# Layer A scores: one 80-column product, or three of 32, 32 and 16 columns

## The chip, the cores and the metric

The kernel runs on one core of one Trainium2 chip. Its time is in device microseconds (us); the figure for a kernel is the median of its runs. One execution is also taken by the hardware profiler, and everything said below of single instructions comes from that one. Engines: PE is TensorE's matmul, PEld its weight load, DVE VectorE, ACT ScalarE, POOL GpSimd, SP SyncE, which issues most of the DMAs. In this kernel a product on PE is always a pair of instructions: LDWEIGHTS brings the stationary operand (rows x columns, as in `128*32`), MATMUL streams the moving operand through it (`128x384`: 384 columns).

## The reference

Four layers, A, B, A, B, each added to its input after a layer norm. Layer A is attention with a memory: the 2048 tokens go in 64 segments of 32, one behind the other, and each segment carries 8 memory rows that are the first 8 output rows of the segment before. So a segment can't be finished before the one ahead of it. Layer B is a linear attention over all tokens. The change is in layer A alone, which is (shortened):

```python
for s in range(n_seg):                               # 64 segments of 32 tokens
    h = jnp.concatenate([mem, xs], axis=1)           # 8 + 32 rows, 640 wide
    q = jnp.einsum('btd,dhe->bhte', h, Wq)           # 32 heads of 192
    k = jnp.einsum('btd,dhe->bhte', h, Wk)
    v = jnp.einsum('btd,dhe->bhte', h, Wv)
    scores = jnp.einsum('bhqe,bhke->bhqk', q, k) * scale
    scores = jnp.where(mask[None, None], scores, -1000000000.0)
    p = _softmax(scores, axis=-1)
    o = jnp.einsum('bhqk,bhke->bhqe', p, v)
    o = jnp.einsum('bhte,hed->btd', o, Wo)
    mem = o[:, :M, :].copy()                         # 8 rows for the next segment
    outs.append(o[:, M:, :])
```

The mask lets everyone see the 8 memory rows, and lets a query see a key that does not come after it.

## The kernel before

Before a chain of segments starts, everything that does not depend on the memory rows is computed for all segments at once and kept in DRAM: the queries and keys of the last 8 tokens of each segment (`kqb`) and their values (`vb`). What is left is `A_chain`, the serial part: 64 segments per layer, each of 4 rounds of 8 heads. Even segments take the rounds as 0, 1, 2, 3, odd ones backwards, so that the weights of the turning round can stay. "Round 0" below is the first in time.

**The work of a round on PE**, in the order in which it is written in the segment loop (the loop over `n` at L1302):

- `project` (L1075, its matmul L1092): q, k or v of 32 rows (8 memory rows and 24 tokens). 5 pieces of the contraction, 640 = 5 x 128, times 4 column groups of 32 columns (`tile_position=(0, 32*g)`), each streaming 384 columns: 20 products, in quads.
- `scores` (L1123, matmul L1129): keys of a chunk, all 128 rows and 80 columns wide, are stationary, and the queries of that chunk, 80 columns, stream. 8 products per round, two accumulated for each of four results. The 80 columns are 64 of two heads' own keys (32 rows each) and 16 of the last tokens of both. This matmul names no column group.
- `attend` (L1135, matmul L1142, result `ps_o`) multiplies the weights E with the values, 8 products of 193 columns on four column groups, and `attend_tails` (L1149, L1155, `ps_t`) does it for the last tokens' queries, 4 products.
- `wo_round` (L1193, L1198, `ps_w`) multiplies the outputs of earlier rounds with Wo, in column groups as well; some of it stands between scores and projections as filling.

The order on PE in a segment is: Q, K, V of round 0; then for rounds 0, 1, 2: Q of the next round, scores of this round, (in round 1, 16 products of L1198), K of the next round, `ps_o`, `ps_t` (rounds 0 and 1) or 8 products of L1198 (round 2), V of the next round; then scores of round 3, the tails of round 2, 20 products of L1198, `ps_o` and `ps_t` of round 3, and the last 52 products of L1198. The result `ps_w` is turned by DVE (L1371), added into the next segment's `hT` (L1373), and the next segment's Q starts.

**Beside PE.** ACT copies a projected q or k from PSUM to `raws` (`to_rows`, L1107), DVE turns it into `QK` (`turn_rows`, L1112): `KT` and `QT` are the two halves of that tile. POOL copies the last tokens' queries and keys into the same tile (`extra_kq`, L1069). So scores read columns 0 to 63 from DVE's turn and 64 to 79 from POOL's copy. ACT's exponential (`weigh`, L1218) reads all of the scores' PSUM tile `ps_s` and writes E, which `attend` loads as stationary. DVE takes the reciprocals (L1162, L1166), ACT scales (L1172), DVE turns the result for `wo_round`.

**What sets the order around the change.** The order of instructions is written out by hand (a manual schedule), engine by engine; waits are added from what each tile's writers and readers are. An instruction that needs more than one wait gets a standalone wait instruction ahead of it on its engine.

**Weights.** Not all of layer A's weights stay on the chip. In each segment SP brings seven pieces of 384 KB into `slot` tiles (three of Wq, two of Wk, two of Wv, for the last round) and four of 320 KB of Wo. `PACE` says after which step of a projection each of the eleven may be issued; the last Wv piece is tied to the Q projection of round 2, the last Wo piece to the K projection of round 3. All go through one queue of SP.

Of the kernel before, what the change touches and what calls it, by code (L numbers as in the profile page):

```python
# [125 lines left out]
class Kernel:  # L126
# [876 lines left out]
    def A_chain(self, xn_dram, at_dram, li, load_slot, piece, late_wo, load_both, wo, low):  # L1003
        nc, tc, KC, NSEG = self.nc, self.tc, self.KC, self.NSEG
        scale = float(self.Dh) ** -0.5
        NR = 4
        with tc.tile_pool(name=f"A{li}_ch", reuse_waits="tile", bufs=1) as sp, \
# [4 lines left out]
            KT, QT = QK[:, 0], QK[:, 1]  # L1012
# [110 lines left out]
            def scores():  # L1123

                S = pop.tile([P, 512], F32, name="ps_s", tag="s")
                for x in range(2):
                    for c in range(4):
                        c0 = 160 * x + 80 * (c // 2)
                        nc.tensor.matmul(S[0:80, c0:c0 + 80], lhsT=KT[:, 4 * x + c, :], rhs=QT[:, 4 * x + c, :],  # L1129
                                         start=(c % 2 == 0), stop=(c % 2 == 1), skip_group_check=True)  # L1130
                return S

            pair = [None]
# [79 lines left out]
            def weigh(E_before=None):  # L1213
                S = scores()
                if E_before is not None:
                    attend_tails(E_before, 2)
                E = sp.tile([P, 320], BF16, name="E", tag="E")
                nc.scalar.activation(out=E[0:80, 0:320], in_=S[0:80, 0:320], func=ACT.Exp, scale=scale)  # L1218
                return E
# [249 lines left out]
```

## Time and profile before

| what | value |
|---|---|
| median of 3 runs | 3266.28 us (3250.03 to 3268.61) |
| the profiled execution: span from its first to its last instruction | 3253.7 us |
| mean granted TensorE clock | 0.994 |
| layer A's two chains in the span, about | 178 to 1380 and 1760 to 2997 us |
| L1129: weight loads and products | 4096 and 4096 |
| duration of one L1129 load and product, median | 123 and 207 ns |
| DMA packets, bytes | 325018, 747.58 MB |

How to read the lines that follow: a group line has the source line, the engine, the operation, what it writes and reads by the program's names, the shape (stationary rows*columns, then the moving operand), the count, the busy time, the mean of one, and the idle time of the engine just before with what ended most of it. A line of the order of time has a start, a length, the engine and the group, and in brackets an idle time before it and who ended it. The end of a matmul is modelled and its pipelined tail overlaps the next one, so the pace of products is read from starts. The page holds the span alone, no time around it.

### The profile page before, as it was taken

The page shows a single profiled execution, that of the slowest core. Times are in us where ns is not written, and L with a number is a line of the kernel's source. Part 1 is how long each engine was busy: PE and PEld are TensorE (multiplying, and loading weights), DVE is VectorE, ACT ScalarE, POOL GpSimd, SP SyncE. Part 2 cuts the span into 40 slices and gives each one's busy share as a digit, 9 for nine tenths or more (in the row PEclk, how much of TensorE's full clock was granted, in tenths as well). Part 3 has the DMA queues.
Part 4 walks back from the last instruction along what each step waited for, and adds up shares of the span by engine and source line. Part 5 has one row for each costly group of instructions (what it writes and reads, how often), then busy time and mean ns, then how long its engine had stood idle before and what let it go on. Part 6 is the DMA issues. An engine that isn't in the chain of part 4 may idle for free.

```text
span 3253.7 us, 140890 instructions
## 1 busy us (share of the span) xinstructions
PE 3095.3 (95%) x59424; PEld 1980.2 (61%) x59730; DVE 2208.8 (68%) x5457; ACT 1883.0 (58%) x4481; POOL 1410.7 (43%) x2920
## 2 busy tenths in 40 slices
PE   9989999999999999999999899999999999999999
PEld 7756666666666666555367566666666666665553
DVE  5557777777777777666643577777777777776465
ACT  3346666666666666646433466666666666666453
POOL 3345555555455455430122355555555554554300
PEclk9999999999999999999999999999999999999999
DMA  8977777777777777840385677777777777778400
GB/s 306 372 271 253 256 248 257 232 255 253 236 256 245 244 257 238 285 166 1 113 319 193 240 233 257 248 252 256 242 264 240 259 244 245 255 236 282 149 1 33
DMA packets 325018, 747.58 MB, mean 230 GB/s; under 512 B 65818, under 2 KB 100274, under 8 KB 321314
## 3 DMA queue, kind: packets, MB, share of 16 engines
q1 hardware_dynamic: 254850, 638.55, 56.1%
q0 software_dynamic: 67616, 86.77, 9.7%
q10 hardware_dynamic: 1920, 13.24, 1.0%
q8 instruction: 469, 7.68, 1.0%
q14 instruction: 163, 1.34, 0.1%
HBM read 668.80 MB, written 77.03 MB: 229 GB/s over the span
## 4 chain that ended last, share of the span: by engine, by line
PE 75%; DMA 11%; DVE 8%; issue 3%; ACT 3%; POOL 0%; SPq 0%; PEld 0%; DVEq 0%; POOLq 0%; ACTq 0%
PE ps_qk_q L1092 12%; PE ps_qk_k L1092 12%; PE ps_v L1092 11%; PE ps_w L1198 10%; DMA arena<-in_A_Wv_dram 6%; PE ps_pre L960 6%; PE ps_s L1129 5%; PE ps_o L1142 3%; PE ps_pre L989 3%; PE kv L1424 2%; DVE raws L1371 2%; PE ps_wo L444 2%; DMA Vp<-vb 2%; DMA arena<-wo_rows 2%; DVE hT L1373 2%
## 5 line engine op out<-in xcount | busy, mean ns | idle before, releaser
L1092 PEld LDWEIGHTS <-hT 128*32 128x32 bf16 x30720 | 792.6, 97 | 422.7 <-issue 43.0
L1112 DVE STREAM_TRANSPOSE QK<-raws 128x512 bf16<-128x512 bf16 (+1 forms) x1152 | 730.7, 643 | 207.3 <-ACT raws L1107 166.7
L1092 PE MATMUL ps_qk_q<-arena,hT 128*32 128x384 bf16 x10240 | 510.4, 327 | 38.2 <-DVE hT L1373 31.1
L1069 POOL COPY QK<-kqb 64x192 bf16<-64x192 bf16 x1024 | 350.4, 342 | 380.9 <-PE ps_s L1129 344.3
L1092 PE MATMUL ps_qk_k<-arena,hT 128*32 128x384 bf16 x10240 | 511.7, 328 | 3.1 <-issue 1.2
L1107 ACT ACTIVATE raws<-ps_qk_k 128x512 bf16<-128x512 f32 (+1 forms) x640 | 313.5, 510 | 253.1 <-PE ps_qk_k L1092 253.1
L1092 PE MATMUL ps_v<-arena,hT 128*32 128x384 bf16 x8192 | 435.2, 326 | 15.2 <-DMA arena<-in_A_Wv_dram 7.2
L1073 POOL DMA_DIRECT2D Vp<-vb x512 | 257.6, 503 | 416.3 <-PE ps_t L1155 252.0
L1172 ACT ACTIVATE raws<-ps_o,rc 128x192 bf16<-128x192 f32 x1024 | 373.4, 420 | 109.3 <-DVE rc L1166 104.8
L1107 ACT ACTIVATE raws<-ps_qk_q 128x512 bf16<-128x512 f32 x512 | 305.7, 597 | 164.5 <-PE ps_qk_q L1092 153.4
L1198 PE MATMUL ps_w<-arena,under 128*32 128x320 bf16 x6144 | 307.4, 300 | 16.7 <-issue 13.1
L1062 POOL DMA_DIRECT2D kqb<-kqb x512 | 290.6, 568 | 70.2 <-POOL QK L1069 50.2
L1121 DVE CAST Vp<-ps_v 64x384 bf16<-64x384 f32 x512 | 286.4, 559 | 37.9 <-ACT Vp L1119 22.8
L1129 PEld LDWEIGHTS <-QK 128*80 128x80 bf16 x4096 | 195.8, 121 | 161.4 <-issue 157.3
L1119 ACT ACTIVATE Vp<-ps_v 64x384 bf16<-64x384 f32 x512 | 246.4, 481 | 55.5 <-PE ps_v L1092 54.2
L1129 PE MATMUL ps_s<-QK 128*80 128x80 bf16 x4096 | 256.8, 210 | 5.4 <-POOL QK L1069 2.8
L1218 ACT ACTIVATE E<-ps_s 80x320 bf16<-80x320 f32 x512 | 217.6, 425 | 32.3 <-PE ps_t L1155 28.9
L1051 ACT ACTIVATE wh<-ps_w 64x160 f32<-64x160 f32 x256 | 76.6, 299 | 264.8 <-DVE raws L1371 254.9
L1058 POOL DMA_DIRECT2D attn<-under x128 | 91.6, 716 | 292.8 <-DVE under L1054 289.7
L960 PEld LDWEIGHTS <-arena 128*128 128x128 bf16 x1920 | 188.4, 98 | 32.4 <-DVE next_xT L97 4.6
L97 DVE CAST arena<-ps_pre 128x512 bf16<-128x512 f32 (+1 forms) x160 | 102.2, 646 | 143.5 <-PE ps_pre L960 96.4
L1142 PE MATMUL ps_o<-Vp,E 80*32 80x193 bf16 x4096 | 180.3, 248 | 13.2 <-DMA Vp<-vb 3.7
(159 smaller groups left out, 4586.2 us busy)
## 6 DMA issues: line engine op xcount, KB each, us to landing
arena<-wo_rows SPq DMA_DIRECT2D x560, 320.0 KB, 5.6
arena<-in_A_Wq_dram SPq DMA_DIRECT2D x427, 384.0 KB, 4.3
arena<-in_A_Wk_dram SPq DMA_DIRECT2D x298, 384.0 KB, 4.8
arena<-in_A_Wv_dram SPq DMA_DIRECT2D x290, 384.0 KB, 6.0
kqb<-kqb POOLq DMA_DIRECT2D x512, 48.0 KB, 4.9
vb<-arena POOLq DMA_DIRECT2D x128, 97.0 KB, 6.1
Vp<-vb POOLq DMA_DIRECT2D x512, 24.2 KB, 4.0
kqb<-arena SPq DMA_DIRECT2D x8, 1536.0 KB, 10.0
```

Source lines behind the costliest of these rows:

```text
L960: nc.tensor.matmul(ps[:, T * i:T * i + T], lhsT=w[b][:, P * c:P * c + P], rhs=xBT[:, b, :], start=(b == 0), stop=(b == KC - 1))
L1062: nc.gpsimd.dma_start(out=kqb[:], in_=self.kqb_d[r, :, s, :])
L1069: nc.gpsimd.tensor_copy(out=o, in_=kqb[h, :].rearrange("p (x c q) -> p x c q", c=3, q=16))
L1073: nc.gpsimd.dma_start(out=Vs[n % 2][64:80, :], in_=self.vb_d[s, r].rearrange("g t f -> (g t) f"))
L1092: last = nc.tensor.matmul(o, lhsT=hT[:, b, :], rhs=rhs, start=(i == 0), stop=(i == KC - 1), tile_position=(0, 32 * g), skip_group_check=True)
L1107: nc.scalar.activation(out=raw[:, c], in_=ps[:, c], func=ACT.Copy)
L1112: nc.vector.transpose(out=o, in_=i)
L1121: nc.vector.tensor_copy(out=o, in_=i)
L1129: nc.tensor.matmul(S[0:80, c0:c0 + 80], lhsT=KT[:, 4 * x + c, :], rhs=QT[:, 4 * x + c, :], start=(c % 2 == 0), stop=(c % 2 == 1), skip_gro ...
L1142: nc.tensor.matmul(O[G][32 * h:32 * h + 32, VH * G:VH * G + 193], lhsT=E[0:80, 80 * h + 32 * G:80 * h + 32 * G + 32], rhs=V[0:80, VH * h:V ...
L1172: nc.scalar.activation(out=out, in_=i, func=ACT.Copy, scale=rc[G])
L1198: step = nc.tensor.matmul(W[q:q + 32, 0:320], lhsT=OT[i // 6][:, i % 6 // 2, 32 * (i % 2):32 * (i % 2) + 32], rhs=rhs, start=(first and i ...
```

## The change

Each 80-column product of `scores` is split into three: stationary columns 0 to 31, 32 to 63 and 64 to 79, each on its own column group and each writing its own rows of the same PSUM tile. All three stream the same 80 query columns. The first two hold the two heads' own keys, the third the last tokens' keys. Result, PSUM tile, accumulation over the two chunks and readers stay.

```diff
                 for x in range(2):
                     for c in range(4):
                         c0 = 160 * x + 80 * (c // 2)
-                        nc.tensor.matmul(S[0:80, c0:c0 + 80], lhsT=KT[:, 4 * x + c, :], rhs=QT[:, 4 * x + c, :],
-                                         start=(c % 2 == 0), stop=(c % 2 == 1), skip_group_check=True)
+                        for g, m in enumerate((32, 32, 16)):
+                            nc.tensor.matmul(S[32 * g:32 * g + m, c0:c0 + 80], lhsT=KT[:, 4 * x + c, 32 * g:32 * g + m],
+                                             rhs=QT[:, 4 * x + c, :], start=(c % 2 == 0), stop=(c % 2 == 1),
+                                             tile_position=(0, 32 * g), skip_group_check=True)
                 return S
```

No other line of the kernel differs.

## The prediction

> **What bounds the kernel now.** I read the page's busy shares, then its chain, then PE's order of time around one block of scores, then ACT's, then the waits of the products behind the scores, then DMA shares over one segment.
>
> ```profile
> PE 3095.3 (95%) x59424; PEld 1980.2 (61%) x59730; DVE 2208.8 (68%) x5457; ACT 1883.0 (58%) x4481; POOL 1410.7 (43%) x2920
> ...
> PE 75%; DMA 11%; DVE 8%; issue 3%; ACT 3%; POOL 0%; SPq 0%; PEld 0%; DVEq 0%; POOLq 0%; ACTq 0%
> PE ps_qk_q L1092 12%; PE ps_qk_k L1092 12%; PE ps_v L1092 11%; PE ps_w L1198 10%; DMA arena<-in_A_Wv_dram 6%; PE ps_pre L960 6%; PE ps_s L1129 5%; PE ps_o L1142 3%; PE ps_pre L989 3%; PE kv L1424 2%; DVE raws L1371 2%; PE ps_wo L444 2%; DMA Vp<-vb 2%; DMA arena<-wo_rows 2%; DVE hT L1373 2%
> ...
> L1129 PE MATMUL ps_s<-QK 128*80 128x80 bf16 x4096 | 256.8, 210 | 5.4 <-POOL QK L1069 2.8
> ```
>
> PE bounds it, but 6% of the chain is the streamed Wv: a second bound lies close. Scores are 5%. What a block costs is read from starts, since busy time counts pipelined tails:
>
> ```profile
> 1003.58 0.99 PE L1092 MATMUL ps_v<-arena,hT 128*32 128x384 bf16 x20
> 1004.39 0.99 PE L1092 MATMUL ps_qk_q<-arena,hT 128*32 128x384 bf16 x20
> 1005.31 0.50 PE L1129 MATMUL ps_s<-QK 128*80 128x80 bf16 x8
> 1005.73 1.00 PE L1092 MATMUL ps_qk_k<-arena,hT 128*32 128x384 bf16 x20
> 1006.56 0.34 PE L1142 MATMUL ps_o<-Vp,E 80*32 80x193 bf16 x8
> 1006.73 0.26 PE L1155 MATMUL ps_t<-Vp,E 80*32 80x193 bf16 x4
> 1006.81 0.34 PE L1092 MATMUL ps_v<-arena,hT 128*32 128x384 bf16 x4
> ```
>
> A projection of 20 takes 0.81 us to the next start when another projection or a 193-wide product follows, 0.92 when scores follow; the scores take 0.42. In single records (medians over 118 inner segments): entry gap 0.104 us (0.916 against 0.812); eight score starts about 0.038 apart, the second 0.059 after the first; then 0.135 from the last score start to the next product, of which 0.038 is its own, so an exit gap of 0.098. Both gaps stand in all four rounds, and the exit is the same before projections, output products and tails. The entry gap can't be the DVE wait there: in rounds 1 and 2 the keys are ready 0.417 us before the first score. So I read both as the array running empty between full-width (80 columns) and 32-column work; 32-column work of other widths follows other 32-column work with no gap.
>
> **The change, part by part.** *Products.* 512 blocks (4 rounds x 64 segments x 2 layers) of 8 loads and 8 products become 24 and 24. No row shows 80-wide products on three column groups, so bounds: four groups run at once on the other rows (384 wide: a quad each 0.1625 us; 193 wide: 0.0825; thus 2.4 columns per ns plus 2 ns), which gives 80/2.4 + 2 = 36 ns per triple; from above, the present 80-column pair's 38 ns (its load is more than twice as wide) is near, and three 21 ns shares of a ps_o quad (63 ns) far. I take 36: it scales the same form of work. A block is then 8 x 0.036 = 0.288 instead of 0.428, and both gaps go (the exit is inside the 0.428): 0.104 + 0.140 = 0.244 us. Projections straight behind scores, 0.823 now, become 0.812 (rounds 0 and 2).
>
> *Waits.* In the built programs, PE's standalone wait ahead of a block (x512 on L1129) is now for DVE's turned keys; after the change it is for the scores before last written, over 110 instructions earlier, and the DVE wait sits on the first weight load. In round 0 the standalone wait ended 0.122 us before the first score, so it would have held the start; a wait carried by a load (E's, at L1142) releases it 0.05 us after its releaser. DVE ends 0.162 (round 0) and 0.147 to 0.274 (round 3) before the present first score, so a start 0.104 earlier still fits. Only PE's own order stands behind that wait.
>
> *What is late next: E.* ACT's order of time around the same block, and last the wait of the ps_o loads (us, times):
>
> ```profile
> 1005.43 0.60 ACT L1107 ACTIVATE raws<-ps_qk_q 128x512 bf16<-128x512 f32 x1 [0.33 <-PE ps_qk_q L1092]
> 1005.92 0.42 ACT L1218 ACTIVATE E<-ps_s 80x320 bf16<-80x320 f32 x1
> ...
>   ACT E L1218: 35.1, 112
> ```
>
> ACT evicts Q first, so in rounds 0 to 2 the exponential starts behind that, not behind the scores: faster scores do not bring E. The first ps_o product starts 0.214 (round 0), 0.71 (1), 0.139 (2) after E's end, and could start 0.054 after it. So round 0 keeps 0.16 of its 0.255, round 1 all 0.244, round 2 0.085. In round 3 E waits for the tails' products (L1155), which move with PE, so all 0.244. Sum 0.733 us per segment, 128 segments: 94 us, if weights were there.
>
> *Weights.* They are not: stretches of one segment, which starts at 1001.94, and last PE's wait in it:
>
> ```profile
> 1003.44:1006.44 3.00, 3.00 (x76) 1.91 (x72) 2.37 (x4) 2.21 (x5) 1.50 (x4) 1.00 0.88 276
> 1006.44:1009.44 3.00, 3.00 (x84) 2.04 (x80) 2.37 (x6) 2.31 (x6) 1.55 (x4) 1.00 0.96 343
> 1009.44:1012.44 3.00, 3.00 (x83) 1.92 (x76) 2.09 (x6) 2.06 (x6) 1.41 (x3) 1.00 0.97 300
> 1012.44:1015.94 3.50, 2.91 (x60) 1.58 (x60) 2.96 (x7) 2.19 (x7) 1.76 (x4) 1.00 1.00 371
> 1015.94:1020.30 4.36, 3.74 (x100) 2.56 (x100) 1.78 (x6) 1.65 (x4) 2.38 (x6) 1.00 0.29 93
> ...
> 1016.48 0.35 PE L1092 MATMUL ps_v<-arena,hT 128*32 128x384 bf16 x4 [0.65 <-DMA arena<-in_A_Wv_dram]
> ```
>
> The next to last number is the DMA share: from 1.5 to 14 us into the segment the engines are full, with the eleven loads of the segment, and PE waits for the last Wv. Over 118 segments that load is issued at 6.23 and lands at 12.5 (median; 5 to 95%: 11.8 to 13.9); its product would start at 12.72 unhindered. The last wo load lands at 16.5, its use is unhindered at 16.54. Loads land about 1.0 us apart with four or five under way, so earlier issues hardly bring earlier landings. I replay each segment: V's use 0.50 earlier (rounds 0 to 2), the wo use a further 0.244, neither before its landing plus 0.04. Landings unmoved: 0.34 us kept per segment; all 0.1 earlier: 0.43; earlier by the whole shift of their issue (0.16 to 0.4): 0.57. The dips in the DMA share before 12.5 us add up to 0.4 us, of which earlier issues can fill a part, so I take 0.39. Were PE's gain only half, it would still be 0.25 to 0.32, since weights clip it.
>
> *Elsewhere.* ACT, DVE and POOL issue what they did. POOL's key copies (L1069) wait for the scores and come earlier; they end 0.8 us or more ahead of the next block. PE's program grows by 16,384 of some 119,000 instructions; its fetch queue moves 7.68 MB at 1.0% of the DMA engines, so 0.14% more: 0.02 us of a segment's full stretch, hidden where PE isn't waiting and at most 3 us in all; taken as nothing.
>
> **Sum.** 128 x 0.39 = 50 us: the profiled execution's span goes from 3253.7 to 3204. The page gives no time around its span; the three timed runs (3250 to 3269) have their median 12.6 us above it, and I carry that over: 3266 - 50 = **3216 us**.
>
> **Rivals.** *(a) Weights take it all.* PE's small loads (Vp, kqb) come earlier too and share the full queues, or triples go every 45 to 50 ns. For: 11% DMA in the chain, a share of 1.00. Against: many segments wait for nothing (the shortest period is 17.93 us against a mean of 18.52). 0.15 to 0.25 us per segment: 19 to 32 us, about 3240.
> *(b) Landings follow their issues*, 0.57 or more: 73 up to the uncapped 94 us, 3193 to 3172. For: the dips. Against: issue to landing of 6 us with the engines full.
> *(c) PE can't be fed.* 48 instructions must go in 0.288 us, 6 ns each. Standalone waits of L1129 and L1142 lie 1.147 us apart in round 1 with 88 loads and products between, 0.839 in round 2 with 56: 12.5 to 14 ns each if that is the sequencer's pace. A block would last 48 x 12.5 = 0.60 us, up to 0.67, against 0.428 + 0.104 now: +0.07 to +0.14, times 512 is 35 to 72 us, **slower: 3301 to 3338**. It decides from 11 ns per instruction, or 22 per product with its load. For: ps_o and ps_t, 21 ns per product, are the densest row. Against: those are as long as their 193 columns need; within a quad the starts of load and product lie 1.7 ns apart; and with the DVE wait off the standalone instruction, PE can read ahead through the projections, which use an instruction per 20 ns.
> The Trainium skill (TensorE: Matmul & The Clock Gate, "Wait — 56ns, not 53.3ns?") speaks against the change: warm matmuls never start closer than about 25 ns, however narrow. By it a block is 24 x 25 = 600 ns, an estimate from that page, and the time is that of (c). The trace does not agree across column groups: neighbours of a quad start 3.4 ns apart.
> *(d) The change doesn't take place:* the built order has 24 products in all 512 blocks, so no chance.
>
> **Chances.** Forecast 0.55, its own range 3190 to 3235; (a) 0.20; (b) 0.10; (c) 0.15. One per cent (33 us) is about what measurement tells from no change: faster 0.65, within 0.20, slower 0.15. The range runs from 3180, which leaves out the far half of (b), to 3275, which leaves out nearly all of (c).
>
> **What would show it.** Right: projection to first score 0.81; block 0.29, so 0.81 + 0.29 from Q's start to K's where 1.34 stands; ps_s products in triples; E waits of L1142 grow from 35 us (112 times) to more in rounds 0 and 2; waits for Wv and wo grow by 0.3 us per segment. Wrong: score starts evenly 20 to 28 ns apart (c); triples wider than 45 ns; a Wv landing that moves with its issue (b); a gap that stays at the block's edges, which would mean that it was not the change of width.

## The result: 2.9% slower

The changed kernel takes 3352.6 us (median of four runs, 3346.3 to 3358.0) against 3264.8 for the kernel before (four runs): a ratio of 1.0287 with a 95% interval of 1.0247 to 1.0326. The forecast was 3216 us, so not only the size but the sign was wrong, and the time lies outside the range. Its profiled execution took 3349.7 us, with a span of 3348.0 at a granted clock of 0.988, against a span of 3253.7 at 0.994 before: the two profiles lie 94 us apart where the medians lie 88 apart, so they show what is to be explained.

The page of the changed kernel: busy shares, the queue that brings PE's instructions, the chain of work, and four groups of PE (busy us, mean ns of one | idle us just before them and what ended most of it).

```profile
PE 3036.8 (91%) x67616; PEld 2112.6 (63%) x67922; DVE 2211.1 (66%) x5457; ACT 1900.5 (57%) x4481; POOL 1413.0 (42%) x2920
...
q8 instruction: 533, 8.73, 1.1%
...
PE 73%; DVE 9%; issue 8%; DMA 6%; ACT 5%; POOL 0%; SPq 0%; DVEq 0%; PEld 0%; ACTq 0%; POOLq 0%
...
L1092 PE MATMUL ps_qk_k<-arena,hT 128*32 128x384 bf16 x10240 | 548.8, 327 | 30.9 <-issue 26.2
...
L1092 PE MATMUL ps_v<-arena,hT 128*32 128x384 bf16 x8192 | 456.1, 328 | 30.5 <-issue 27.2
...
L1200 PE MATMUL ps_w<-arena,under 128*32 128x320 bf16 x6144 | 347.6, 305 | 53.0 <-issue 51.1
...
L1130 PE MATMUL ps_s<-QK 128*32 128x80 bf16 (+1 forms) x12288 | 256.3, 203 | 50.8 <-issue 47.2
```

PE is busy for 59 us less, as it was meant to be, and yet the span is longer: PE now stands still. In the chain the share of DMA fell from 11% to 6%, and "issue", time in which an engine waited for nothing that the profile shows, rose from 3% to 8%. It has spread over PE's groups: the scores wait 47.2 us for it where all their idle time was 5.4 us before.

PE's order of time, from one segment that has such a stall and from the next one:

```profile
1007.39 0.45 PE L1130 MATMUL ps_s<-QK 128*32 128x80 bf16 x22
1010.00 0.21 PE L1130 MATMUL ps_s<-QK 128*32 128x80 bf16 x2 [2.15 <-issue]
...
1018.20 0.99 PE L1092 MATMUL ps_qk_q<-arena,hT 128*32 128x384 bf16 x20
1019.01 0.39 PE L1130 MATMUL ps_s<-QK 128*32 128x80 bf16 x18
1019.21 0.34 PE L1092 MATMUL ps_qk_k<-arena,hT 128*32 128x384 bf16 x1
1019.23 0.24 PE L1130 MATMUL ps_s<-QK 128*32 128x80 bf16 x6
1019.30 0.98 PE L1092 MATMUL ps_qk_k<-arena,hT 128*32 128x384 bf16 x19
1020.20 0.35 PE L1144 MATMUL ps_o<-Vp,E 80*32 80x193 bf16 x8
```

The lower six lines are the change as it was forecast: 0.81 us from Q's start to the first score instead of 0.92, and 0.29 from there to the bulk of K instead of 0.42. In single records triples go 36 ns apart. The upper two are what was not forecast: in the middle of a block, behind 22 of its 24 products, PE waits 2.15 us. No semaphore, engine or weight is named as what ended that wait. What ended shortly before it is seen in the transfers of the same time. The DMA view from 1007.5 to 1008.6 us (queue: packets, MB, share of the 16 DMA engines in this window):

```profile
q1 hardware_dynamic: 155, 0.35, 81.7%
q0 software_dynamic: 26, 0.04, 11.3%
q8 instruction: 1, 0.02, 6.1%
```

This one packet of the instruction queue has 16,384 bytes. It started at 1007.525 and ended at 1008.591, and PE went on at 1010.00, 1.41 us later. The queue's 533 packets stand against 136,452 records of PE and its weight loads, 256 to a packet, and by the built program's order 194 of the 234 stalls counted below end at instruction 194 or 195 modulo 256. **PE had run out of instructions.**

From the same records one can read how a fetch goes: in the runs without streamed loads (below) a packet starts 0.8 us or less (medians) after PE passes into the block of 256 that it already has, so I take that passing as the moment at which the next packet is asked for. The times between, as medians by the place in a segment at which the packet starts (before / after):

| place of the packet's start | PE passes the border until the packet starts | packet | 256 instructions last |
|---|---|---|---|
| 1.5 to 4 us | 0.44 / 0.69 us | 0.96 / 0.95 | 5.25 / 4.13 |
| 4 to 8 us | 1.98 / 1.74 | 0.96 / 0.97 | 5.03 / 4.20 |
| 8 to 12 us | 2.82 / 2.85 | 0.96 / 0.97 | 5.37 / 5.26 (with the stalls in it) |

After the packet's end PE needs 1.3 us more at the least (5th percentile; 1.4 is the median where PE waits). With the DMA engines full that makes 2.8 + 1.0 + 1.3 = 5.1 us for a fetch, and 1.98 + 0.96 + 1.3 = 4.2 a little earlier. Before the change 256 instructions lasted 5.0 to 6.0 us, barely longer than a fetch. It added 128 instructions to a segment's 848, just where they are the densest, and 256 of them last as little as 3.5 us.

**The count.** I count a stall where PE's starts lie over 0.25 us apart, the waiting instruction has no wait of its own, and the gap ends 1.1 to 1.8 us after a packet of the instruction queue ended. Before: 119 stalls, 81 us. After: 234, 261 us, thus 180 us more. Where hardly any fetch is late (the experiments without streamed loads), the same rule still counts 18 and 34 us, so it has some noise in it, and 16 of the 180 us may be no more than that. Some of the expectations below use a narrower count, of those stalls alone that end at instruction 194 or 195 and less 0.15 us each: 52 us before and 217 after.

The stretches of the segment that starts at 1015.75 (us; busy time of PE, PEld, DVE, ACT, POOL; clock; DMA share; GB/s) and its wait for the last Wv:

```profile
1020.25:1023.25 3.00, 3.00 (x106) 2.44 (x107) 2.60 (x6) 2.56 (x6) 1.69 (x5) 1.00 0.99 360
1023.25:1026.25 3.00, 3.00 (x105) 2.88 (x100) 2.29 (x7) 2.22 (x6) 1.28 (x4) 1.00 0.98 280
```

```profile
1028.34 0.35 PE L1092 MATMUL ps_v<-arena,hT 128*32 128x384 bf16 x4 [0.18 <-DMA arena<-in_A_Wv_dram]
...
1031.22 0.31 PE L1200 MATMUL ps_w<-arena,under 128*32 128x320 bf16 x2 [1.49 <-issue]
```

The engines are as full as before, and the fetch has to share them: this segment loses 0.18 us to a weight and 1.49 to its own instructions.

### The profile page after: what moved, and what is told of

It is laid out like the page before. It is cut to its first block, busy times and chain, and to the rows that moved or that the text cites. A ratio compares the mean times of both kernels' runs of the same rounds, so it can differ in the third digit from the quotient of the medians.

```text
span 3348.0 us, 157267 instructions
## 1 busy us (share of the span) xinstructions
PE 3036.8 (91%) x67616; PEld 2112.6 (63%) x67922; DVE 2211.1 (66%) x5457; ACT 1900.5 (57%) x4481; POOL 1413.0 (42%) x2920
## 3 DMA queue, kind: packets, MB, share of 16 engines
q1 hardware_dynamic: 254850, 638.55, 54.7%
## 4 chain that ended last, share of the span: by engine, by line
PE 73%; DVE 9%; issue 8%; DMA 6%; ACT 5%; POOL 0%; SPq 0%; DVEq 0%; PEld 0%; ACTq 0%; POOLq 0%
PE ps_qk_q L1092 12%; PE ps_qk_k L1092 12%; PE ps_v L1092 11%; PE ps_w L1200 9%; PE ps_pre L960 6%; DMA arena<-in_A_Wv_dram 4%; PE ps_o L1144 3%; PE ps_s L1130 3%; PE ps_pre L989 3%; ACT raws L1174 2%; PE kv L1426 2%; DVE raws L1373 2%; PE ps_wo L444 2%; DVE hT L1375 2%; PE ps_pq L495 1%
## 5 line engine op out<-in xcount | busy, mean ns | idle before, releaser
L1092 PEld LDWEIGHTS <-hT 128*32 128x32 bf16 x30720 | 936.1, 97 | 368.8 <-issue 107.5
L1092 PE MATMUL ps_qk_k<-arena,hT 128*32 128x384 bf16 x10240 | 548.8, 327 | 30.9 <-issue 26.2
L1092 PE MATMUL ps_qk_q<-arena,hT 128*32 128x384 bf16 x10240 | 520.3, 327 | 39.0 <-DVE hT L1375 30.5
L1092 PE MATMUL ps_v<-arena,hT 128*32 128x384 bf16 x8192 | 456.1, 328 | 30.5 <-issue 27.2
L1200 PE MATMUL ps_w<-arena,under 128*32 128x320 bf16 x6144 | 347.6, 305 | 53.0 <-issue 51.1
L1130 PE MATMUL ps_s<-QK 128*32 128x80 bf16 (+1 forms) x12288 | 256.3, 203 | 50.8 <-issue 47.2
L1130 PEld LDWEIGHTS <-QK 128*32 128x32 bf16 (+1 forms) x12288 | 213.9, 96 | 120.3 <-issue 57.1
L1200 PEld LDWEIGHTS <-under 128*32 128x32 bf16 x6144 | 195.0, 98 | 68.4 <-issue 64.9
L1144 PE MATMUL ps_o<-Vp,E 80*32 80x193 bf16 x4096 | 201.1, 253 | 38.1 <-issue 23.3
```

Of the source, the lines that this page charges most:

```text
L1092: last = nc.tensor.matmul(o, lhsT=hT[:, b, :], rhs=rhs, start=(i == 0), stop=(i == KC - 1), tile_position=(0, 32 * g), skip_group_check=True)
L1130: nc.tensor.matmul(S[32 * g:32 * g + m, c0:c0 + 80], lhsT=KT[:, 4 * x + c, 32 * g:32 * g + m], rhs=QT[:, 4 * x + c, :], start=(c % 2 == 0) ...
L1144: nc.tensor.matmul(O[G][32 * h:32 * h + 32, VH * G:VH * G + 193], lhsT=E[0:80, 80 * h + 32 * G:80 * h + 32 * G + 32], rhs=V[0:80, VH * h:V ...
L1200: step = nc.tensor.matmul(W[q:q + 32, 0:320], lhsT=OT[i // 6][:, i % 6 // 2, 32 * (i % 2):32 * (i % 2) + 32], rhs=rhs, start=(first and i ...
```

## The experiments

The theories: **F**, PE stalls for its instructions, because 256 of them now last less than a fetch does under the streamed loads; **D**, the dense scores themselves are at fault (PE's sequencer, as in rival (c)); **W**, the weights have become the bound, since everything before them moved.

**More instructions, same scores.** The kernel before, with weight loads that nobody needs:

```diff
                     for g in range(4):
...
+                        if g % 2:
+                            nc.tensor.ldweights(hT[:, b, :], tile_position=(0, 32 * g))
                         last = nc.tensor.matmul(o, lhsT=hT[:, b, :], rhs=rhs, start=(i == 0),
```

> Kernel before, with a second, needless weight load ahead of every second product of a projection (120 more PE instructions per segment, where the change adds 128; scores untouched). Theory F (PE waits for its instructions: 256 at a time come by DMA, and with the weights' loads filling the DMA engines a fetch takes 4.7 to 5.2 us): quads of a projection stay 0.162 us apart, but 256 instructions now last about 4.9 us instead of 5.5, so PE stalls at instruction numbers that are 194 or 195 mod 256 grow from 52 us in all to 130 to 200, and the time is 80 to 150 us longer: 3345 to 3415. Theory D (what hurts is the dense burst of 48 instructions inside a block of scores): no burst is added, within 10 us of before. Theory W (faster scores only run into late weights): nothing is faster, so within 10 us of before.

3359.1 us (3356.9 to 3361.3, two runs), a ratio of 1.0286 [1.025, 1.0322]: as slow as the changed kernel, with not one score touched. Its groups of PE:

```profile
L1094 PE MATMUL ps_qk_k<-arena,hT 128*32 128x384 bf16 x10240 | 528.9, 329 | 32.1 <-issue 26.7 <-ACT E L1220 2.0 <-DMA arena<-in_A_Wk_dram 1.5
...
L1094 PE MATMUL ps_v<-arena,hT 128*32 128x384 bf16 x8192 | 449.7, 329 | 24.7 <-issue 23.1 <-DMA arena<-in_A_Wv_dram 1.4
...
L1200 PE MATMUL ps_w<-arena,under 128*32 128x320 bf16 x6144 | 317.6, 303 | 22.0 <-issue 20.2 <-DMA arena<-wo_rows 1.5
...
L1131 PE MATMUL ps_s<-QK 128*80 128x80 bf16 x4096 | 257.9, 210 | 27.0 <-issue 21.5 <-POOL QK L1069 2.7 <-DVE raws L1287 1.1
```

The same idle time for "issue" stands on the same four groups, and no wait for weights there is above 3 us. Stalls by the count: 160 us, 79 more than before. The loads cost a little of their own: round 0's scores start 0.096 us later, and by the output products of round 2 a segment is 0.112 us behind, 14 us in all. D and W fall.

**No streamed loads.** Both kernels without the eleven loads that a segment streams. The core of the edit; `release` asks each held load whether it would start a transfer, and drops those that would:

```diff
             if holds.get((m, b)) != r:
                 holds[m, b] = r
+                if self.dry:
+                    return None
                 self.last_load = nc.sync.dma_start(out=slot[m, b], in_=wview[m][:, b, PW * r:PW * r + PW])
```

> Kernel before without the eleven streamed weight loads of each segment (it computes with the weights that lie there, so the output is another). The base for the next run. Theory F: with the DMA engines nearly empty a fetch takes about 2.7 us, no PE stall at 194 or 195 mod 256 is left, and no weight is late: segments at the shortest period of before, 17.9 us instead of 18.5, so 75 us faster than before, about 3190. Theory W: the same, since no weight can be late. Theory D: stalls without a named releaser stay as before.

> Kernel after without the eleven streamed weight loads of each segment (output as said for the kernel before it). Theory F: the stalls go, and what is left is what the split saves on PE, 0.73 us per segment by the sum of the prediction: 94 us below the unstreamed kernel before, about 3095. Theory D: the stalls do not depend on the DMA, so it stays 50 to 90 us above the unstreamed kernel before. Theory W: also 94 us below it, but then the kernel after should have shown longer waits for weights, not stalls without a releaser.

3155.7 us without the change and 3093.9 with it (two runs each; ratios to the kernel before 0.9663 [0.963, 0.9697] and 0.9474 [0.9442, 0.9507]). With the DMA engines nearly idle (a share of 0.15 between 300 and 1300 us of the changed kernel without these loads, against 0.71 with them) the same 128 instructions more make the kernel 62 us **faster**. The groups of PE with the change (output products of the scores L1154, here waiting for Vp):

```profile
L1102 PE MATMUL ps_v<-arena,hT 128*32 128x384 bf16 x8192 | 433.2, 326 | 0.0
L1210 PE MATMUL ps_w<-arena,under 128*32 128x320 bf16 x6144 | 323.7, 300 | 3.3 <-issue 2.8 <-DMA arena<-wo_rows 0.5
L1140 PE MATMUL ps_s<-QK 128*32 128x80 bf16 (+1 forms) x12288 | 235.2, 202 | 3.6 <-POOL QK L1079 3.3
L1154 PE MATMUL ps_o<-Vp,E 80*32 80x193 bf16 x4096 | 189.8, 250 | 27.5 <-DVE Vp L1131 24.8 <-DMA Vp<-vb 2.6
```

The issue stalls are gone from V (27.2 us to none), from `ps_w` with `under` (51.1 to 2.8) and from the scores (47.2 to none). So it takes both: more instructions, and transfers in the way of the fetch. It is also the clean price of the change on PE: 0.57 us of a segment (17.93 to 17.37), where 0.733 was forecast. By rounds: the output products of round 0 start 0.162 us earlier, those of round 1 0.495, those of round 2 0.493, and round 3 adds only 0.073.

**One round at a time.** The split in round 3 alone, and in round 0 alone (32 instructions per segment more instead of 128):

```diff
-            def scores():
+            def scores(n):
...
-                        nc.tensor.matmul(S[0:80, c0:c0 + 80], lhsT=KT[:, 4 * x + c, :], rhs=QT[:, 4 * x + c, :],
-                                         start=(c % 2 == 0), stop=(c % 2 == 1), skip_group_check=True)
+                        for g, m in enumerate((32, 32, 16) if n in (3,) else (80,)):
+                            nc.tensor.matmul(S[32 * g:32 * g + m, c0:c0 + 80], lhsT=KT[:, 4 * x + c, 32 * g:32 * g + m],
+                                             rhs=QT[:, 4 * x + c, :], start=(c % 2 == 0), stop=(c % 2 == 1),
+                                             tile_position=(0, 32 * g) if n in (3,) else None, skip_group_check=True)
```

> The split in round 3 alone (32 more PE instructions per segment instead of 128), where E waits for PE and not for ACT. Theory F: PE saves 0.24 us per segment less what late weights take back, 15 to 25 us; 32 more instructions bring the next fetch forward by 0.5 us at about 13 us into the segment, where the next fetch falls into the stretch with the DMA engines emptying: little lost. 3240 to 3265. Theory D: a burst still stalls PE once per segment, a quarter of the loss: 3265 to 3290.

> The split in round 0 alone (32 more PE instructions per segment). It saves 0.16 us per segment on PE, 20 us in all uncapped. Theory F: its 32 instructions bring the fetches between 4 and 15 us forward by up to 0.5 us, as those of round 3 did (stalls +34 us by instruction numbers, time +30 us with 0.08 us per segment saved): 3265 to 3290. Were it the block's burst itself that stalls, round 0 would lose as much as round 3: 3290.

Round 3: 3292.5 us, 1.009 [1.0062, 1.0117]; 30 us slower, where I had expected 3240 to 3265 by F; the time alone lies nearer to D's 3265 to 3290. The stalls grew by 43 us, and the gain, by the kernels without streamed loads, is 0.073 us of a segment: 9 us. Round 0: 3238.9 us, 0.9941 [0.9918, 0.9963], **faster than both kernels**; the stalls did not grow (82.6 against 81.5 us), and the shortest segment fell from 17.93 to 17.78. Both runs missed what I had expected, in opposite directions: for round 3 I had taken the DMA engines to be emptying where its fetch falls, and for round 0 I had then charged each instruction what it cost in round 3. Round 0's block stands at 3.3 us of a segment. The stretches of 256 that PE enters in the 5 us ahead of it have their next packet start 0.7 us after the border (median of the run with round 0 split); with 1.3 us behind the packet a fetch takes 3.0 us and the stretch lasts 4.5. Round 3's stands at 13 us: ahead of it, in the run with round 3 split, the packet starts 2.8 us after the border, and the fetch takes 5.1 us where the stretch lasts 5.4, and in 40% of these stretches nothing is spare (28% before the split).

**Later loads.** If F holds, a segment with fewer loads under way at a time has shorter fetches. Six of the eleven loads of a segment are released one place later, in the kernel before and in the changed one, and in the changed one later still (seven loads, another table of the same kind; the edit of the first two is shown):

```diff
-PACE = {("Q", 0): 0, ("K", 0): 1, ("V", 0): 3, ("Q", 1): 4, ("K", 1): 4, ("V", 1): 3, ("Q", 2): 1, ("K", 2): 0, ("V", 2): 0,
-        ("Q", 3): 0, ("K", 3): 0}
+PACE = {("Q", 0): 0, ("K", 0): 1, ("V", 0): 3, ("Q", 1): 4, ("K", 1): 4, ("Q", 2): 4, ("K", 2): 0, ("V", 2): 0,
+        ("Q", 3): 0, ("K", 3): 0, ("V", 3): 0}
```

> Kernel before with the last six of a segment's eleven streamed loads tied to later steps (one place of the pacing table each, about 0.9 us), scores untouched. Theory F with a queue (a fetch of instructions waits behind the weight loads that are under way, four to five of them): with one load fewer under way the wait from PE's entering a stretch of 256 instructions to the start of the next fetch falls from 2.8 to about 2.0 us at 8 to 15 us of a segment, and the fetch stalls (75 to 85, 50 to 60 us) halve; the last weights come later by up to 0.3 us per segment. The two about cancel: 3235 to 3275. Theory F without a queue (engines that are full delay a fetch alike however many loads are under way): stalls as before, weights later, 3265 to 3300.

> Kernel after with the same later pacing. Theory F with a queue: fetch stalls (200, some 217 us) fall to 100 to 140 us, 3255 to 3310. Theory F without a queue: stalls as in the kernel after, 3350 to 3380.

> Kernel after with seven loads tied to steps later still (two loads fewer under way). Theory F with a queue: the wait for a fetch falls to about 1.3 us and stalls to under 80 us, but the last Wv and Wo now land up to 0.7 us later per segment: 3240 to 3320. Theory F without a queue: 3370 to 3430.

The kernel before: 3281.1 us, 1.0069 [1.0042, 1.0095]. The changed one: 3292.6, 1.0112 [1.0078, 1.0146], so 60 us are won back of the 88; still later: 3313.9, 1.0186 [1.0149, 1.0223]. The wait for a packet's start at 8 to 12 us of a segment fell from 2.82 to 1.59 us in the kernel before, and from 2.85 to 2.18 and 2.01 in the changed one; the stalls fell from 81 to 45, and from 261 to 186 and 179. So the fetch does wait for the streamed loads, the longer the more of them are under way. The time of the kernel before, 3281, lies in the range that I had given for F without a queue; what speaks for the queue are the waits for the packets and the stalls, though with the latest loads these did not fall to the 1.3 us and the 80 us that I had expected. But the last wo load lands later too, at 17.1 instead of 16.5 us in the kernel before, and what the fetch gains the weights lose: there the chain of work gives 18% to DMA, where it was 11%.

**Does the place alone decide?** Loads without use again, 32 per segment, in one place each, and the scores untouched: ahead of the projections around round 0's scores (shown), or ahead of the last V projection.

```diff
+                        for _ in range(1 if m != "V" and n == 1 and i < 4 else 0):
+                            nc.tensor.ldweights(hT[:, b, :], tile_position=(0, 32 * g))
```

> The kernel before with 32 needless weight loads per segment (4,096 in all, as many instructions as the split of one round adds): one ahead of each of the first 16 products of Q and of K next to round 0's scores. The scores keep their 80 columns, so PE gains nothing. Theory P (the place decides: here the fetch of PE's instructions starts 0.4 us after PE asks and 256 instructions last over 5 us, so up to 2 us are spare): 3255 to 3272, within 0.3% of the kernel before, fetch stalls near its 52 us. Theory U (each added instruction costs the same wherever it stands: a quarter of the 97 us that 120 loads per segment cost): 3284. Theory S (the split of round 0 alone came out well because of its scores, and 32 more instructions there cost what they cost in round 3): 3290 or more.

> The same 32 needless loads per segment, put ahead of the products of the last V projection, just before round 3's scores, where the fetch of PE's instructions waits 2.8 us with the DMA engines full. Theory P: the added fetch stalls of the split of round 3 alone (about 35 us) without its small gain of about 10: 3290 to 3310. Theory U: 3284, the same as with the loads in round 0. If what the split of round 3 lost had nothing to do with the number of instructions but with its scores or tails: 3262, as before.

Round 0: 3301.8 us, 1.0146 [1.0121, 1.0171]. Round 3: 3324.4, 1.0209 [1.0189, 1.0228]. The first is 30 us above P's range and agrees with S (3290 or more) by its time; the second is above every theory. Neither time comes from what I was testing: the stalls by the count are 86 and 93 us, only 5 and 12 more than before. In the first, the output products of round 0 start 0.16 us of each segment later (20 us) and the waits of L1144 for Vp's transfer grew by 10. In the second, two rows of the waits (us, times, longest) show what was late:

```profile
ACT Vp L1121 <- PE ps_t L1157: 91.4, 97, 2.4
...
PE ps_o L1144 <- DVE Vp L1123: 54.7, 89, 0.7
```

The copy of the V rows starts only behind the tails' products, and the output products of round 3 wait for it, 54.7 us, where all waits of the output products for Vp were 4.0 us before. That and the 12 us of stalls are the whole 67. The trace's semaphore updates show why the copy is late, though in the built program it waits for V's last product as before. In these runs each needless load, and each product of the projections that have them, updates PE's semaphore, where otherwise only the last product of a projection does: 14,151 and 12,867 updates against 6,215. No two of them lie closer than 30 ns, and beside such a projection they follow each other every 30 to 34 ns. In the second run one V projection ends at 1024.69, the updates go on to 1025.50, and the copy starts at 1025.52. Over all segments it starts 0.88 us (median) after V's last product, where it was 0.05; in the first run the copies of Q and K beside round 0's scores start 0.37 us after the last product instead of 0.05, which fits the 0.16 us above. The 120 loads of the first experiment have this too (38,081 updates): the copies start 0.1 us later there, which fits its 0.112 us of a segment. These two runs say nothing for or against the place; that rests on the split kernels alone.

**Two rounds.**

> Scores split in rounds 0 and 1 only, 64 more instructions per segment. Without fetch stalls the two rounds save 0.16 and 0.244 us of a segment: 52 us, 3210. Theory P: round 1's block stands 7 us into the segment, where a fetch waits 2.0 us instead of 0.4, so a part of its 31 us goes back to stalls: 3225 to 3250, no clear step beyond the 3239 of round 0 alone. Theory U (24 us per 32 instructions): 3258, as before.

The edit is that of one round with (0, 1) in place of (3,). 3262.5 us (twelve runs), 1.0012 [0.9994, 1.003]: nothing left. The shortest segment is 17.52 us, 0.41 less than before, which would be 52 us; the stalls are 130 us, 49 more. Round 1's block at 7 us costs what it brings. P had 3225 to 3250 here and U 3258, so this time does not speak for P; what does is that round 0's 32 instructions added 1 us of stalls and round 3's 43.

**Fewer instructions for the same columns.** 64 columns on two column groups and 16 on a third:

```diff
-                        for g, m in enumerate((32, 32, 16)):
+                        for g, m in ((0, 64), (2, 16)):
```

> In all rounds the 80 columns go as two products, 64 columns on two column groups and 16 on a third: 64 more instructions per segment instead of 128. If the gaps at a block's edges go for any width that is one of whole groups, PE saves as much as with three products, and half of the fetch stalls that the change added come (about 80 us instead of 165): 3270 to 3295. If a width of 64 columns costs the gaps as a width of 80 does, the stalls stand alone: 3310 to 3340.

4041.9 us, 1.2413 [1.2392, 1.2435], far from both cases. PE's order of time around a block:

```profile
1005.67 1.00 PE L1092 MATMUL ps_qk_q<-arena,hT 128*32 128x384 bf16 x20
1006.61 2.36 PE L1130 MATMUL ps_s<-QK 128*64 128x80 bf16 x16
1008.76 0.74 PE L1200 MATMUL ps_w<-arena,under 128*32 128x320 bf16 x16
```

A block of 16 products takes 2.158 us (median) instead of 0.428. Nearly all of it, 2.155, are the 15 steps from one start to the next, 0.144 each (0.153 from 64 columns to 16, 0.133 back); the next product starts 0.003 after the last 16 columns, with no gap. A product of 80 columns took 0.038 before; by that the change of width, 64 to 16 or back, costs about 0.106. A block's entry cost 0.104 in the kernel before, and its exit 0.098. I read this as the prediction's mechanism on its own: the gaps belong to each change of width, 32 columns and fewer being one width. The Trainium skill (TensorEngine Tiling (Array Packing), Key Properties) states that changing the tiling mode drains the engine; if that is what happens here, these three numbers are its price. The run has a use for F as well: a segment lasts 24.8 us, the transfers have time, a fetch starts 0.6 us after it is asked for at 8 to 12 us of a segment, and the stalls are 12 us with 64 instructions more.

**The sum.** If stalls and PE's gain are all, then what a kernel differs by from the one before (medians of the same runs) is the growth of the stalls less the gain:

| kernel | stalls, us | more than before | PE's own | sum | measured |
|---|---|---|---|---|---|
| the change | 261 | +180 | -72 (0.57 x 128) | +108 | +88 |
| needless loads, 120 | 160 | +79 | +14 (0.112 x 128) | +93 | +97 |
| round 3 | 124 | +43 | -9 (0.073 x 128) | +34 | +30 |
| round 0 | 83 | +1 | -20 (0.154 x 128) | -19 | -22 |
| rounds 0 and 1 | 130 | +49 | -52 (0.41 x 128) | -3 | +5 |
| the change, loads later | 186 | +104 | -72 | +32 | +32 |

It closes within 20 us everywhere and within 8 in all but the changed kernel. There some stalls may fall into time in which PE would have waited for a weight anyhow: its waits for Wv and wo fell by 9 us (7.2 to 2.5, and 9.4 to 5.3); the rest of the 20 us is open. The table leaves out the two kernels where weights came later and little was won (before with loads later: -36 by stalls, +21 measured; the change with the latest loads: +26 and +53), and the runs whose time has another cause, above.

It also leaves out the clock. In layer A's chains the granted clock of the changed kernel falls to a half in 16 stretches, 58 us together, against two with 6.8 us before. 12 of the 16 begin between 0.2 us before and 0.7 us after the end of a stall of over 1 us. One follows the stall shown above (the stretch, with the clock third from the end; then the same 24 products in it and a segment later):

```profile
1010.67:1014.08 3.41, 3.41 (x66) 2.65 (x59) 1.02 (x4) 0.90 (x3) 2.92 (x6) 0.50 0.18 37
...
1011.62 1.87 PE L1200 MATMUL ps_w<-arena,raws 128*32 128x320 bf16 x24
...
1031.73 1.01 PE L1200 MATMUL ps_w<-arena,raws 128*32 128x320 bf16 x24
```

Over the whole span the time at half clock is 82 us against 37.5, so it costs at most 22 us, half of the difference (an estimate: as if PE's clock had set the pace in all of it); for the 120 needless loads, with 61 us, at most 12. In the changed kernel's sum that would make the open 20 us up to 42, so the stalls by the count are more than what the path lost by them.

## Why the prediction was wrong, step by step

*Products: right.* Triples lie 36 ns apart, and a block takes 0.285 to 0.29 us. The Trainium skill's rule (TensorE: Matmul & The Clock Gate, "Wait — 56ns, not 53.3ns?") that starts never lie less than about 25 ns apart does not hold across column groups here: 36 ns for three are 12 each. Rival (c)'s sequencer never showed: score starts come in triples.

*The gaps are the change of width: right* as far as tested, and borne out by the 64 and 16 columns.

*Waits: right.* The scores start 0.812 us after Q, so the turned keys are no later than the start.

*E is late next: right in sum, not in place.* E's waits grew as forecast:

```profile
  ACT E L1220: 99.4, 314
```

The row had 35.1 us, 112 times. Rounds 0 to 2 keep 0.493 us without streamed loads, where 0.16 + 0.244 + 0.085 = 0.489 was forecast. But round 1 alone brings 0.333 and round 2 nothing: in round 1 the products behind the scores gain about 0.1 more than the two gaps (below), and by round 2 the scores' lead has run out against E.

*Round 3: wrong.* I let it keep all 0.244 since "E waits for the tails". Round 3's output products wait for the V rows first (ACT's copy, then DVE's cast: 24.8 us in the row without streamed loads, where it is L1131), and those hang on the V projection ahead of the scores, not on the scores. It keeps 0.073. The four rounds bring 72 us uncapped, not 94.

*Weights: right that landings do not follow issues.* The changed kernel can't show it: its last Wv is issued at 6.07 us instead of 6.23 and lands at 12.4 instead of 12.5. But in the kernel before with later loads it is issued 1.7 us later, at 7.96, and lands 0.2 us earlier, so rival (b) had no ground. Wrong was that they would set what is kept: the waits for Wv and wo were to grow by 0.3 us per segment and fell, and DMA's share of the chain fell from 11% to 6%, since PE, held up by its own instructions, came to its weights later and not earlier.

*The step that failed* is the one under "Elsewhere": that the program's growth by 16,384 instructions and the fetch queue at 1.0% of the DMA engines were "taken as nothing", 3 us at most. I priced the fetch by its bytes. Its price is its delay: one block of 256 instructions, asked for only when the block before it is begun, 4.2 to 5.1 us in the middle of a segment, against 3.5 to 5 us that PE takes to run a block. That is 180 us of stalls by the count. They were in the profile before as well, 81 us of them; one stands in the segment that I worked out, a line above the wait for Wv that I quoted:

```profile
1015.07 0.76 PE L1092 MATMUL ps_v<-arena,hT 128*32 128x384 bf16 x6 [0.41 <-issue]
```

I read 3% of "issue" in the chain and passed on. The Trainium skill has a section that should have been weighed (Runtime: NRT & Kernel Launch, Instruction fetch mechanics): it states that instructions come in blocks of 16 KiB, 256 of them, from a DMA queue of the sequencer's own, and that this is mostly hidden. The trace agrees on the block (16,384 bytes), and not on the hiding.

*Rival (c)* had nearly the time (3301 to 3338) and the sign, by the wrong mechanism: PE could not be fed, but the supply that failed was the transfer of its instructions and not the sequencer's pace, as 62 us gained without streamed loads show. Its chance of 0.15 was for another story.

## What to carry to other kernels

A program that is unrolled and dense pays for each instruction by its place: before splitting one product into three, count how long PE needs for 256 instructions there, and compare it with a fetch under the load of that stretch (here 2.7 us with little under way, about 5 with the DMA engines full). Idle time for "issue" that ends 1.3 to 1.5 us after a packet of the instruction queue is the sign to look for, even at 3% of the chain. A saving that costs instructions is worth having where the fetch has time to spare: here round 0 alone, 3239 us, beats both kernels, and all four rounds lose.

## What the runs showed of the hardware that I had not expected

- PE's instructions come 256 at a time in packets of 16,384 bytes. The next one starts when PE has entered the block that it holds: 0.8 us later or less when little else moves (medians by place, without streamed loads), 2.8 us later with the DMA engines at a share of 0.96 to 1.00, takes 1.0 us, and can be used 1.3 us after its end.
- A column group that has no work runs ahead of the others. The scores use three of four; in the timeline one product of the next projection starts ahead of the last six scores that precede it in the program, with 0.02 us between (1019.21 and 1019.23). I take it to be that of the fourth group. The products behind a block gain 0.07 to 0.1 us, which I put down to it.
- Alternating products of 64 and 16 columns pays about 0.106 us at each change of width, where products of 32 and 16 columns in the dense triples follow each other at 12 ns each without any.
- Updates of PE's semaphore lie 30 ns apart or more. Where every product and load updates it, an engine that waits for the last product starts late: ACT's copy 0.88 us after it with 32 needless loads, against 0.05 before (medians).
- The granted clock falls to 0.50 for 3.41 us at a time (once for 6.83), in 12 of 16 cases in the changed kernel's chains at the end of a stall of over 1 us; most stalls of that length are not followed by it.
